# Decayed attention and a gated FFN: one ring of PSUM banks for values and FFN, and RMS weights put into the FFN weights after group 0

## The chip, the cores and the metric

The kernel runs on one core of one Trainium2 chip. The metric is the device time of one execution in microseconds; a kernel is run several times and the median counts.

## The reference

Eight batches of eight heads, 576 tokens, head size 64. Attention adds a decay, the difference of cumulated logs of `f`, to causal scores; its output, put together over the heads, is normalised by its root mean square and goes through a gated FFN.

```python
scores = scale * np.matmul(q, k.transpose(0, 1, 3, 2))
log_f = np.log(np.clip(f, 0.0001, 1.0))
cum = np.cumsum(log_f, axis=-1)
decay = cum[:, :, :, None] - cum[:, :, None, :]
scores = np.where(causal, -1000000000.0, scores + decay)
attn = softmax(scores)                       # over the keys
x = np.matmul(attn, v)                       # -> (8 * 576, 512)
...
rms = np.sqrt(np.mean(x * x, axis=-1, keepdims=True) + 1e-06)
xn = x / rms * rms_g
g = xn @ w_gate                              # 512 -> 1536
silu = g * (1.0 / (1.0 + np.exp(-g)))
out = silu * (xn @ w_val) @ w_out            # 1536 -> 512
```

All inputs and the output are float32; the kernel multiplies in bf16.

## The kernel before, in words

**Tiling.** A batch has four row blocks of 128 tokens and a last one of 64 (`qi` 0 to 4). For each block and each key block up to it, TensorE makes scores of all eight heads into a double PSUM bank (`sc`, 128 x 1024), ScalarE takes the exponent into SBUF (`PT`, or `P` for the last key block), and GpSimd puts zeros over the causal corner (`affine_select`). `values` then multiplies these with `Vs`, the v rows scaled by their decay with the scale itself as a 65th column, into one bank for the even heads and one for the odd heads (`par` 0 and 1). VectorE takes the reciprocal of the 65th column (`rden`) and writes the quotient to `x`. `norm` forms the root mean square on ScalarE and GpSimd and writes `xn` in bf16. The rows are then transposed into `xT`: by TensorE for the first two batches (a PSUM bank and a copy by VectorE per piece), by DMA for the others.

**FFN groups.** A group is 512 rows: the four full blocks of a batch, groups 0 to 7; group 8 collects the eight last blocks (`xTr`). `gate` takes one bank for the product with `wg` and one for that with `wv`, ScalarE makes the tanh (`th`), VectorE makes `ga` from `th` and the first bank, which frees that bank, and then `hT` from `ga` and the second bank, which frees the other. Groups 0 and 1 run piece by piece (one row block, four column chunks in one bank, sixteen 128 x 128 matmuls); the others one column chunk of 128 at a time over 512 rows. `project` adds up twelve matmuls in one bank, ScalarE copies it, SP stores it.

**PSUM.** The eight banks are: four in `sc` (two double banks), one `po` for values, three `ff` for everything else. In batch 0 the odd heads' values use `ff`. When the last score (or the last value) has been taken, the banks of `sc` and `po` are handed to the ring `ff` (`heir`), so the last groups have up to eight.

**RMS weights.** `rms_g` is folded in at two places. Groups 0 and 1 multiply it into their `xT` pieces while copying them from PSUM. After each third of group 1's gates, `weigh` multiplies it into that third of `wg` and `wv` in place (four VectorE multiplies of 128 x 512 for each of the two, called a pack below), for groups 2 to 8. A third of the columns has the index `i`.

**Order.** Nothing is issued in the order of the loops. Every step is a unit with an engine, an assumed duration, a key and dependencies; `Plan.run` plays them through and gives each engine, whenever it is free, the ready unit of the smallest key whose ring slots are free. Keys get a small random offset from a seeded generator. Each engine then runs its units strictly in the planned order. Scores and values are also chained, each to the one before it. `akey` spreads batch b's attention over the FFN of group b - 1, and `qkey` sets the keys of the first two batches by hand. Loads of v, and most of q and k, are issued by GpSimd (POOL), transposes by DMA and stores by SP.

Of the kernel before, what the change touches and what calls it, by code (L numbers as in the profile page):

```python
# [32 lines left out]
class Plan:  # L33

    def __init__(self, rings, fifo, heir):
        self.units, self.fifo, self.heir = [], fifo, heir
        self.free = {name: list(range(n)) for name, n in rings.items()}
        self.left = {name: [] for name in rings}  # L40
# [24 lines left out]
    def end_of(self, u):  # L65
        for h in u.give:
            h.n -= 1
            if h.n == 0:
                if h.ring in self.heir and not self.left[h.ring]:
                    to, slots = self.heir[h.ring]  # L70
                    self.free[to] += slots(h.slot)
                else:
                    self.free[h.ring].append(h.slot)
        for v in u.then:
            v.need -= 1
            if v.need == 0:
                self.ready[v.eng].append(v)

    def run(self):
# [67 lines left out]
def fox_ffn_kernel(ctx, tc, q, k, v, f, moe_w_gate, moe_w_val, moe_w_out, moe_rms_g, out):  # L147
    nc = tc.nc
# [14 lines left out]
    def ring(name, n, shape, dt, pool=sb):  # L163
        return [pool.tile(shape, dt, name=f"{name}{i}") for i in range(n)]

    sizes = dict(qk2=4, qk=12, QT=3, v32=4, Vs=2, PT=8, P4=2, x=6, xn=4, xT=2, xTr=1, hT=2, th=2, ga=2, ores=3,
                 sc=2, po=1, ff=3, hw=8, sw=8)
    T_qk2 = ring("qk2", sizes["qk2"], [128, H, 2, D], BF16)
# [15 lines left out]
    T_sc = ring("sc", sizes["sc"], [128, 2, 512], F32, ps)  # L184
    T_po = ring("po", sizes["po"], [128, 512], F32, ps)
    T_ff = ring("ff", sizes["ff"], [128, GT], F32, ps)
    n_ff, n_sc = sizes["ff"], sizes["sc"]
    T_ff += [t[:, i, :] for t in T_sc for i in range(2)] + T_po

# [15 lines left out]


    P = Plan(sizes, {"v32", "qk", "qk2", "QT", "Vs", "PT", "x", "xn"}, {"sc": ("ff", lambda i: [n_ff + 2 * i, n_ff + 2 * i + 1]),
                     "po": ("ff", lambda i: [n_ff + 2 * n_sc + i])})

# [122 lines left out]
    def load_w(i, key):  # L332
        c0, c1 = i * 512, (i + 1) * 512
        for w, src, nm in ((wg, moe_w_gate, "g"), (wv, moe_w_val, "v")):
            def emit(w=w, src=src):
                nc.gpsimd.dma_start(out=w[:, :, c0:c1], in_=src[:, c0:c1].rearrange("(c p) f -> p c f", p=128))
            Lw[nm, i] = load("POOL", 0.75, (512, 0.0061), key, emit, late=2.6)

    def weigh(i, key, deps):

        c0, c1 = i * 512, (i + 1) * 512
        for w, nm in ((wg, "g"), (wv, "v")):
            def emit(w=w):
                for dc in range(NDC):
                    nc.vector.tensor_scalar_mul(w[:, dc, c0:c1], w[:, dc, c0:c1], rgT[:, dc:dc + 1])  # L345
            Lw[nm, i] = dve(1.14, key, emit, deps)

# [131 lines left out]

    def bank_of(h):  # L480
        return T_ff[h.slot] if h.ring == "ff" else T_po[h.slot]

    hold_x, evac, last_val = {}, {}, [None]

    def values(b, qi, key):
        p0, n = rows(qi)
        hx = hold_x[b, qi] = Hold("x", 1)
        for par in range(2):
            hpo = Hold("ff" if b == 0 and par == 1 and qi < LAST else "po", 1)

# [30 lines left out]
    def norm(b, js, key):  # L521
# [15 lines left out]
        for i, j in enumerate(js):  # L537
# [6 lines left out]
            if g < 2:  # L544
# [9 lines left out]
                def cp(hf=hf, g=g, c=c):  # L554
                    tp = T_ff[hf.slot].bitcast(BF16)[:, 0:512].rearrange("p (c t) -> p c t", t=128)
                    nc.vector.tensor_tensor(T_of[g][hold_xT[g].slot][:, :, c:c + 128], tp, bcast(rgT, 128), ALU.mult)
                pieces[b, j] = dve(0.65, key - 0.02, cp, [t, L_rg], take=[hold_xT[g]], give=[hf])
            else:
# [37 lines left out]
    def gate(g, key, deps, i, pairs):  # L596
# [114 lines left out]
```

## Time and profile before

| | |
|---|---|
| runs | 401.74, 398.55, 401.13 us (median 401.13) |
| profiled execution | 398.83 us, of which the span is 396.7 us |
| TensorE busy | 365.8 us, 92% of the span |
| VectorE, ScalarE, GpSimd busy | 225.0, 237.7, 196.8 us |
| packs of RMS weights (L345) | 12 + 12 multiplies, 10.9 + 6.0 us, from 85.8 to 124.2 us |
| chain that ended last | TensorE 78%, DMA 7%, VectorE 7%, GpSimd 4% |

The profile names engines PE (TensorE), PEld (its weight loads), DVE (VectorE), ACT (ScalarE), POOL (GpSimd) and SP. Times are in microseconds from the start of the span. A busy TensorE is the bound here; idle time of another engine costs something only where TensorE waits for it.

### The profile page before, as it was taken

Reading aid. Unit: us, or ns where it says so; the run is one execution under the profiler, and the core shown is the slowest. Engines: PE = TensorE matmul, PEld = TensorE weight load, DVE = VectorE, ACT = ScalarE, POOL = GpSimd, SP = SyncE. Lnnn points to the kernel's source line nnn. Section 1 sums busy time; section 2 is a strip of 40 time slices with the busy share of each in tenths; the row PEclk is TensorE's granted clock in tenths of the full one; section 3 lists DMA queues with packets and bytes.
Section 4 is the critical chain, followed back from the end, with each engine's and each line's share of the span. In section 5 each row is a group of like instructions: output and inputs, shape, how many; then the busy total and the mean of one; then the engine's idle time right before and its main releaser. Section 6 shows DMA issues by size and latency. Waiting matters only on the chain.

```text
span 396.7 us, 9672 instructions
## 1 busy us (share of the span) xinstructions
PE 365.8 (92%) x3941; PEld 217.4 (55%) x3941; DVE 225.0 (57%) x456; ACT 237.7 (60%) x377; POOL 196.8 (50%) x275
## 2 busy tenths in 40 slices
PE   2668999997699999899999999999999999999995
PEld 1567898785496554554455544554555444444442
DVE  4555787478968555564565555645555554455530
ACT  4655588786647955786677657865885532232212
POOL 8862469997839945695398456841211100000000
PEclk9998999999979999999999999999999999999998
DMA  9999999999829999899799999992120210001004
GB/s 132 189 200 190 199 143 162 176 175 168 141 39 109 187 158 122 103 154 154 78 122 168 161 112 82 190 150 55 32 57 28 55 33 28 26 26 55 26 28 106
DMA packets 133708, 44.83 MB, mean 113 GB/s; under 512 B 122432, under 2 KB 127040, under 8 KB 133664
## 3 DMA queue, kind: packets, MB, share of 16 engines
q0 software_dynamic: 76000, 22.16, 59.2%
q1 hardware_dynamic: 57136, 22.05, 30.7%
q8 instruction: 31, 0.51, 0.6%
q10 hardware_dynamic: 528, 0.00, 0.2%
q14 instruction: 13, 0.11, 0.1%
HBM read 37.90 MB, written 9.44 MB: 119 GB/s over the span
## 4 chain that ended last, share of the span: by engine, by line
PE 78%; DMA 7%; DVE 7%; POOL 4%; issue 2%; ACT 1%; SPq 0%; ACTq 0%; POOLq 0%
PE ff L605 35%; PE ff L630 17%; PE po L498 7%; PE sc L605 6%; PE sc L451 6%; PE sc L630 5%; DMA v<-in_v_dram 4%; DMA xT<-xn 3%; PE po L605 2%; DVE wg L345 1%; DVE wv L345 1%; DVE hT L612 1%; DVE ga L619 1%; POOL qk L303 1%; DVE x L514 1%
## 5 line engine op out<-in xcount | busy, mean ns | idle before, releaser
L469 ACT ACTIVATE PT<-sc 128x1024 bf16<-128x1024 f32 x96 | 95.2, 1018 | 22.6 <-PE sc L451 22.5
L605 PE MATMUL ff<-xT,wg 128*128 128x128 bf16 (+1 forms) x628 | 88.8, 290 | 5.9 <-DVE ga L619 3.2
L605 PE MATMUL ff<-xT,wv 128*128 128x128 bf16 (+1 forms) x636 | 90.7, 288 | 1.0 <-DVE hT L612 0.8
L619 DVE SCALAR_TENSOR_TENSOR ga<-th,ff 128x512 f32<-128x512 f32 x87 | 59.2, 683 | 49.2 <-ACT th L617 48.8
L630 PE MATMUL ff<-wo,hT 128*128 128x512 bf16 x336 | 86.1, 379 | 0.0
L605 PEld LDWEIGHTS <-wg 128*128 128x128 bf16 x720 | 55.9, 102 | 42.4 <-issue 6.3
L617 ACT ACTIVATE th<-ff 128x512 f32<-128x512 f32 x87 | 51.5, 595 | 44.6 <-PE ff L605 32.8
L605 PEld LDWEIGHTS <-wv 128*128 128x128 bf16 x720 | 54.9, 100 | 36.6 <-issue 1.8
L612 DVE SCALAR_TENSOR_TENSOR hT<-ga,ff 128x512 bf16<-128x512 f32 x94 | 63.7, 683 | 18.7 <-PE ff L605 16.7
L630 PEld LDWEIGHTS <-hT 128*128 128x128 bf16 x432 | 40.1, 98 | 45.1 <-issue 1.3
L476 POOL TENSOR_SCALAR_AFFINE_SELECT PT<-PT 128x1024 bf16<-128x1024 bf16 x32 | 35.4, 1106 | 58.0 <-ACT PT L469 57.7
L498 PEld LDWEIGHTS <-PT 128*128 128x128 bf16 x896 | 38.4, 99 | 17.3 <-issue 4.8
L498 PE MATMUL po<-Vs,PT 128*128 128x65 bf16 x856 | 41.1, 196 | 3.2 <-DVE x L514 2.4
L426 POOL TENSOR_TENSOR Vs<-v,decT 128x512 bf16<-128x512 f32 (+1 forms) x30 | 31.7, 1057 | 12.8 <-DMA v<-in_v_dram 12.2
L451 PE MATMUL sc<-QT,KT 64*128 64x128 bf16 (+1 forms) x960 | 34.6, 214 | 3.0 <-ACT PT L469 1.4
L512 DVE RECIPROCAL rden<-po 128x4 f32<-128x4 f32 (+1 forms) x76 | 13.5, 177 | 40.7 <-PE po L498 40.5
L451 PEld LDWEIGHTS <-KT 64*128 64x128 bf16 x960 | 25.0, 97 | 19.4 <-issue 14.9
L530 ACT ACTIVATE junk<-x 128x512 bf16<-128x512 f32 (+1 forms) x40 | 25.1, 627 | 14.7 <-DVE x L514 14.6
L514 DVE TENSOR_TENSOR x<-po,rden 128x256 f32<-128x256 f32 (+1 forms) x76 | 32.1, 423 | 2.6
L326 POOL DMA_DIRECT2D v<-in_v_dram x34 | 30.4, 896 | 0.1
L303 POOL DMA_DIRECT2D qk<-in_q_dram x34 | 30.1, 885 | 0.8 <-POOLq L695 0.8
L542 ACT ACTIVATE xn<-x,rs 128x512 bf16<-128x512 f32 (+1 forms) x40 | 27.2, 714 | 5.4 <-POOL rs L535 5.3
(76 smaller groups left out, 306.1 us busy)
## 6 DMA issues: line engine op xcount, KB each, us to landing
out_dram<-ores SPq DMA_DIRECT2D x32, 256.0 KB, 2.4
v<-in_v_dram POOLq DMA_DIRECT2D x27, 256.0 KB, 5.3
qk<-in_q_dram POOLq DMA_DIRECT2D x26, 128.0 KB, 5.9
qk<-in_k_dram POOLq DMA_DIRECT2D x26, 128.0 KB, 5.7
wg<-in_moe_w_gate_dram POOLq DMA_DIRECT2D x3, 512.0 KB, 15.9
wv<-in_moe_w_val_dram POOLq DMA_DIRECT2D x3, 512.0 KB, 17.4
wo<-in_moe_w_out_dram POOLq DMA_DIRECT2D x2, 768.0 KB, 17.6
v<-in_v_dram SPq DMA_DIRECT2D x5, 256.0 KB, 9.9
```

What stands on the lines that cost most here:

```text
L303: nc.gpsimd.dma_start(out=T_qk[h.slot][0:n, :].rearrange("p (h d) -> p h d", d=D), in_=src[b, :, p0:p0 + n, :].rearrange("h p d -> p h d"))
L426: eng.tensor_tensor(T_Vs[hv.slot][0:n, j, :, 0:D], T_v32[h.slot][0:n, :, :], bcast(dj, D), ALU.mult)
L451: nc.tensor.matmul(t[:, par, c:c + n], lhsT=kt[r, p, kj * 128:(kj + 1) * 128], rhs=qt[r, p, qi * 128:qi * 128 + n], start=True, stop=True)
L469: nc.scalar.activation(T_of_p[hp.slot][:, 0:2 * half].rearrange("p (a c) -> p a c", a=2)[:, :, 0:cols], T_sc[h.slot][:, :, 0:cols], ACT.Ex ...
L476: nc.gpsimd.affine_select(out=d, in_=d, pattern=[[0, 8], [1, n]], compare_op=ALU.is_ge, fill=0.0, base=0, channel_multiplier=-1)
L498: nc.tensor.matmul(po[:, p, :], lhsT=T_of_p[h.slot][:, c:c + 128], rhs=vs[:, kj, 2 * p + par, :], start=(kj == 0), stop=(kj == qi))
L514: nc.vector.tensor_tensor(d, po[:, :, 0:D], bcast(r, D), ALU.mult)
L605: nc.tensor.matmul(T_ff[h.slot][:, c:c + n], lhsT=w[:, dc, fc * 128:(fc + 1) * 128], rhs=xT[:, dc, t0:t0 + n], start=(dc == 0), stop=(dc = ...
L612: nc.vector.scalar_tensor_tensor(hT, in0=three[0], scalar=0.5, in1=three[1], op0=ALU.mult, op1=ALU.mult)
L617: th = act(0.6, key - 0.1, lambda: nc.scalar.activation(T_th[ht.slot], T_ff[hg.slot], ACT.Tanh, scale=0.5), [ug], take=[ht])
L619: a = dve(0.72, key - 0.1, lambda: nc.vector.scalar_tensor_tensor(T_ga[ha.slot], in0=T_th[ht.slot], scalar=1.0, in1=T_ff[hg.slot], op0=ALU ...
L630: nc.tensor.matmul(T_ff[hf.slot], lhsT=T_hT[hold_hT[g].slot][:, fc, j * 128:(j + 1) * 128], rhs=wo[:, fc, :], start=(fc == 0), stop=(fc == ...
```

## The change

Values take their banks from `ff` in all batches, `po` is gone, and `ff` has four banks to the end: nothing is handed over from `sc`. Group 0 alone multiplies `rms_g` into its `xT` pieces; group 1's pieces become plain copies, and the weights are multiplied between groups 0 and 1, each pack as soon as the four gates of group 0 that read it have been issued. The packs' keys move from 1.25, 1.5, 1.75 to 0.75, 1.0, 1.25, their assumed duration from 1.14 to 1.3. The keys of the 64-row blocks of batches 0 and 1 move from -4.8 and -4.2 to 0.3 and 0.9, and the random seed is another one, so that the plan of all engines is drawn anew.

```diff
     def __init__(self, rings, fifo, heir):
...
-                if h.ring in self.heir and not self.left[h.ring]:
-                    to, slots = self.heir[h.ring]
-                    self.free[to] += slots(h.slot)
-                else:
-                    self.free[h.ring].append(h.slot)
+                self.free[h.ring].append(h.slot)
...
-        draw = random.Random(71)
+        draw = random.Random(149)
...
-                 sc=2, po=1, ff=3, hw=8, sw=8)
+                 sc=2, ff=4, hw=8, sw=8)
...
+    PLAIN = 1
...
     def weigh(i, key, deps):
...
-            Lw[nm, i] = dve(1.14, key, emit, deps)
+            Lw[nm, i] = [dve(1.3, key, emit, deps[nm])]
...
     def values(b, qi, key):
...
-            hpo = Hold("ff" if b == 0 and par == 1 and qi < LAST else "po", 1)
+            hpo = Hold("ff", 1)
...
     def norm(b, js, key):
...
-                    nc.vector.tensor_tensor(T_of[g][hold_xT[g].slot][:, :, c:c + 128], tp, bcast(rgT, 128), ALU.mult)
-                pieces[b, j] = dve(0.65, key - 0.02, cp, [t, L_rg], take=[hold_xT[g]], give=[hf])
+                    to = T_of[g][hold_xT[g].slot][:, :, c:c + 128]
+                    if g < PLAIN:
+                        nc.vector.tensor_tensor(to, tp, bcast(rgT, 128), ALU.mult)
+                    else:
+                        nc.vector.tensor_copy(to, tp)
+                pieces[b, j] = dve(0.69 if g < PLAIN else 0.42, key - 0.02, cp, [t, L_rg], take=[hold_xT[g]], give=[hf])
...
     def qkey(b, qi, ahead=0.0):
         if b < 2:
-            return (2 * b - 9 + 0.2 * (START[qi] + ahead)) if qi < LAST else -4.8 + 0.6 * b + 0.04 * ahead
+            return (2 * b - 9 + 0.2 * (START[qi] + ahead)) if qi < LAST else 0.3 + 0.6 * b + 0.04 * ahead
...
-                if g == 1:
-                    weigh(i, 1 + (i * 4 + 4) / 16, [ended[1, i * 4 + j] for j in range(4)])
+                if g == PLAIN - 1:
+                    weigh(i, PLAIN - 1 + (i * 4 + 12) / 16, {"g": [began[g, i * 4 + j] for j in range(4)],
+                                                             "v": [ended[g, i * 4 + j] for j in range(4)]})
```

What this does to the engines' order is shown at three places. The first is VectorE's queue around the middle packs, among group 1's gates. Before (`ff_124` to `ff_126` are the three `ff` banks, `po_123` the values' bank, `hT_113` holds group 1, `x` rows are the values' evacuations):

```order
L512 RECIPROCAL rden_142<-po_123 128x4
L514 TENSOR_TENSOR x_100<-po_123,rden_142 128x4x64
L612 SCALAR_TENSOR_TENSOR hT_113<-ga_117,ff_126 128x4x128
L345 TENSOR_SCALAR wg<-wg,rgT 128x512 x4
L619 SCALAR_TENSOR_TENSOR ga_116<-th_115,ff_124 128x512
L345 TENSOR_SCALAR wv<-wv,rgT 128x512 x4
L612 SCALAR_TENSOR_TENSOR hT_113<-ga_116,ff_125 128x4x128
```

In the changed kernel three of the packs stand at the turn from group 0 to group 1 (`hT_112` holds group 0, the two `COPY` rows are the first plain xT pieces of group 1, `ff_123` is the fourth bank):

```order
L606 SCALAR_TENSOR_TENSOR hT_112<-ga_117,ff_123 128x4x128
L550 COPY xT_110<-ff_125 128x4x128
L550 COPY xT_110<-ff_126 128x4x128
L338 TENSOR_SCALAR wg<-wg,rgT 128x512 x4
L338 TENSOR_SCALAR wv<-wv,rgT 128x512 x4
L613 SCALAR_TENSOR_TENSOR ga_116<-th_114,ff_125 128x512
L338 TENSOR_SCALAR wg<-wg,rgT 128x512 x4
L502 RECIPROCAL rden_141<-ff_124 128x4
L504 TENSOR_TENSOR x_100<-ff_124,rden_141 128x4x64
```

The other three packs stand further ahead, one by one among group 0's gates; behind the last of group 1's gates there is none any more.

The second place is VectorE's queue in the first 40 us, at the scaling of batch 1's fourth v block (`Vs_88<-v_83`), which waits for a load. Before, with the two evacuations of batch 0's fourth block (`x_102`) behind it:

```order
L612 SCALAR_TENSOR_TENSOR hT_112<-ga_117,ff_125 128x4x128
L426 TENSOR_TENSOR Vs_88<-v_83,decT 128x8x64
L427 CAST Vs_88<-decT 128x8
L619 SCALAR_TENSOR_TENSOR ga_116<-th_114,ff_124 128x512
L512 RECIPROCAL rden_141<-po_123 128x4
L514 TENSOR_TENSOR x_102<-po_123,rden_141 128x4x64
```

Now both evacuations stand ahead of it:

```order
L504 TENSOR_TENSOR x_102<-ff_123,rden_141 128x4x64
L606 SCALAR_TENSOR_TENSOR hT_112<-ga_117,ff_126 128x4x128
L502 RECIPROCAL rden_142<-ff_125 128x4
L504 TENSOR_TENSOR x_102<-ff_125,rden_142 128x4x64
L419 TENSOR_TENSOR Vs_88<-v_83,decT 128x8x64
L420 CAST Vs_88<-decT 128x8
L613 SCALAR_TENSOR_TENSOR ga_116<-th_114,ff_124 128x512
```

The third place is the last gates of group 8 on VectorE. Before, the banks come from `ff`, `sc` and `po`:

```order
L619 SCALAR_TENSOR_TENSOR ga_117<-th_114,po_123 128x512
L619 SCALAR_TENSOR_TENSOR ga_116<-th_115,sc_122 128x512
L612 SCALAR_TENSOR_TENSOR hT_112<-ga_117,ff_126 128x512
L612 SCALAR_TENSOR_TENSOR hT_112<-ga_116,ff_124 128x512
```

Now four banks go round:

```order
L613 SCALAR_TENSOR_TENSOR ga_116<-th_114,ff_124 128x512
L613 SCALAR_TENSOR_TENSOR ga_117<-th_115,ff_123 128x512
L606 SCALAR_TENSOR_TENSOR hT_112<-ga_116,ff_125 128x512
L606 SCALAR_TENSOR_TENSOR hT_112<-ga_117,ff_126 128x512
```

More of the change, by code (lines that the diff above doesn't have):

```diff
@@ L33, with __init__ @@
 class Plan:
-    def __init__(self, rings, fifo, heir):
-        self.units, self.fifo, self.heir = [], fifo, heir
+    def __init__(self, rings, fifo):
+        self.units, self.fifo = [], fifo
         self.free = {name: list(range(n)) for name, n in rings.items()}
@@ L184, in fox_ffn_kernel @@
     T_sc = ring("sc", sizes["sc"], [128, 2, 512], F32, ps)
-    T_po = ring("po", sizes["po"], [128, 512], F32, ps)
     T_ff = ring("ff", sizes["ff"], [128, GT], F32, ps)
-    n_ff, n_sc = sizes["ff"], sizes["sc"]
-    T_ff += [t[:, i, :] for t in T_sc for i in range(2)] + T_po
     wg = sb.tile([128, NDC, DF], BF16, name="wg")
@@ L204, in fox_ffn_kernel @@
     rden = [sb.tile([128, 4], F32, name=f"rden{i}") for i in range(2)]
-    P = Plan(sizes, {"v32", "qk", "qk2", "QT", "Vs", "PT", "x", "xn"}, {"sc": ("ff", lambda i: [n_ff + 2 * i, n_ff + 2 * i + 1]),
-                     "po": ("ff", lambda i: [n_ff + 2 * n_sc + i])})
+    P = Plan(sizes, {"v32", "qk", "qk2", "QT", "Vs", "PT", "x", "xn"})
     def pe(dur, key, emit, deps=(), take=(), give=()):
@@ L336, in emit @@
                 nc.gpsimd.dma_start(out=w[:, :, c0:c1], in_=src[:, c0:c1].rearrange("(c p) f -> p c f", p=128))
-            Lw[nm, i] = load("POOL", 0.75, (512, 0.0061), key, emit, late=2.6)
+            Lw[nm, i] = [load("POOL", 0.75, (512, 0.0061), key, emit, late=2.6)]
     def weigh(i, key, deps):
@@ L478, in score_block @@
                 masked[b, qi].append(pool(0.15 + 0.95 * n / 128, key, mk, [e]))
-    def bank_of(h):
-        return T_ff[h.slot] if h.ring == "ff" else T_po[h.slot]
     hold_x, evac, last_val = {}, {}, [None]
@@ L488, in values @@
         for par in range(2):
-            hpo = Hold("ff" if b == 0 and par == 1 and qi < LAST else "po", 1)
+            hpo = Hold("ff", 1)
             def emit(par=par, hpo=hpo):
-                po = bank_of(hpo)[:, 0:4 * 65].rearrange("p (j d) -> p j d", d=65)
+                po = T_ff[hpo.slot][:, 0:4 * 65].rearrange("p (j d) -> p j d", d=65)
                 vs = T_Vs[hold_Vs[b].slot]
@@ L509, in ev @@
             def ev(par=par, hpo=hpo):
-                po = bank_of(hpo)[0:n, 0:4 * 65].rearrange("p (j d) -> p j d", d=65)
+                po = T_ff[hpo.slot][0:n, 0:4 * 65].rearrange("p (j d) -> p j d", d=65)
                 r = rden[par][0:n, :]
@@ L613, in gate @@
         dur = 0.865 if len(pairs) == 1 else 0.9
-        began[g, len([x for x in began if x[0] == g])] = ug = pe(dur, key, lambda: mm(wg, hg), deps + [Lw["g", i]], take=[hg])
-        uv = pe(dur, key + 0.0001, lambda: mm(wv, hv), [ug, Lw["v", i]], take=[hv], give=[hx])
+        began[g, len([x for x in began if x[0] == g])] = ug = pe(dur, key, lambda: mm(wg, hg), deps + Lw["g", i], take=[hg])
+        uv = pe(dur, key + 0.0001, lambda: mm(wv, hv), [ug] + Lw["v", i], take=[hv], give=[hx])
         ended[g, len([x for x in ended if x[0] == g])] = uv
```

## The prediction

> **What bounds the kernel now.** I read the page's first two parts first, then the span in short windows, then the waits and the timeline of the stretch that stands out.
>
> ```profile
> PE 365.8 (92%) x3941; PEld 217.4 (55%) x3941; DVE 225.0 (57%) x456; ACT 237.7 (60%) x377; POOL 196.8 (50%) x275
> ...
> PE   2668999997699999899999999999999999999995
> ```
>
> TensorE is the bound: 396.7 - 365.8 = 30.9 us of the span is all that waits can give back, plus what a lowered clock costs. Two places hold nearly all of it: the first 45 us, and a hole around slices 9 to 12. The windows below cut the hole (stretch, length, busy us of PE, PEld, DVE, ACT, POOL, then the granted clock, DMA share, GB/s).
>
> ```profile
> 84.00:88.00 4.00, 3.74 (x81) 3.45 (x80) 3.81 (x8) 3.35 (x6) 3.82 (x6) 1.00 1.34 177
> 88.00:92.00 4.00, 3.26 (x57) 2.55 (x55) 3.93 (x8) 3.21 (x6) 3.99 (x6) 1.00 1.75 182
> 92.00:96.00 4.00, 2.35 (x18) 1.03 (x16) 3.93 (x8) 1.41 (x2) 3.04 (x5) 1.00 1.46 160
> 96.00:100.00 4.00, 3.96 (x86) 3.77 (x86) 2.29 (x8) 3.77 (x7) 2.29 (x4) 1.00 1.43 141
> 100.00:104.00 4.00, 4.00 (x77) 2.80 (x74) 3.82 (x3) 3.64 (x7) 3.99 (x7) 1.00 1.09 181
> 104.00:108.00 4.00, 1.32 (x20) 0.63 (x17) 4.00 (x5) 1.55 (x3) 3.40 (x6) 0.95 0.47 111
> 108.00:112.00 4.00, 3.19 (x37) 3.02 (x37) 2.80 (x10) 0.60 (x1) 0.00 (x0) 0.50 0.19 57
> 112.00:116.00 4.00, 4.00 (x54) 4.00 (x52) 2.17 (x4) 1.85 (x5) 2.62 (x5) 0.70 0.01 2
> ```
>
> From 84 to 112 TensorE is busy 21.8 of 28 us: 6.2 idle. VectorE is full there. The clock is 0.50 and then 0.70: 3.19 x 0.5 + 4.00 x 0.3 = 2.8 us more. Together **9.0 us**. Who makes it is in the timeline (start, length, engine, line; in brackets the idle before and its releaser).
>
> ```profile
> 100.99 6.84 DVE L345 TENSOR_SCALAR wg<-wg,rgT 128x512 bf16<-128x512 bf16 x4
> 101.39 1.04 POOL L426 TENSOR_TENSOR Vs<-v,decT 128x512 bf16<-128x512 f32 x1
> 107.75 0.67 DVE L619 SCALAR_TENSOR_TENSOR ga<-th,ff 128x512 f32<-128x512 f32 x1
> 108.47 1.86 PE L605 MATMUL ff<-xT,wg 128*128 128x128 bf16 x16 [3.15 <-DVE ga L619]
> ```
>
> A pack of four weight multiplies (L345) holds VectorE for 6.84 us while GpSimd runs its v multiplies; the gate operation (L619) that frees an ff bank is queued behind it, and TensorE waits 3.15 us and restarts at half speed. The other packs:
>
> ```profile
> 85.84 2.54 DVE L345 TENSOR_SCALAR wg<-wg,rgT 128x512 bf16<-128x512 bf16 x4
> 90.59 3.71 DVE L345 TENSOR_SCALAR wv<-wv,rgT 128x512 bf16<-128x512 bf16 x4
> 120.86 1.13 DVE L345 TENSOR_SCALAR wv<-wv,rgT 128x512 bf16<-128x512 bf16 x4
> 120.94 2.40 POOL L303 DMA_DIRECT2D qk<-in_q_dram  x2
> 123.05 1.53 DVE L345 TENSOR_SCALAR wg<-wg,rgT 128x512 bf16<-128x512 bf16 x4
> ...
> L345 DVE TENSOR_SCALAR wg<-wg,rgT x12: 332/375/4528, 85.8 to 124.2; 128x512 bf16<-128x512 bf16 x12
> ...
> PE po L498 <- DVE x L514: 2.4, 3, 1.6
> ```
>
> The same multiply takes 332 or 4528 ns. Four times the short one, overlapped, make a pack of 1.13; what GpSimd does meanwhile sets the rest (beside loads that it issues, 1.13 and 1.53). The single po bank costs 2.4 us in three waits, all of them behind these packs, so they are in the 9.0 already.
>
> The Trainium skill (SBUF — State Buffer, "Who interferes with whom") says that a VectorE instruction in a two-port mode and a GpSimd instruction exclude each other for a whole instruction; the 4528 ns agree with being locked out by several in a row.
>
> **The change, part by part.** (1) The packs leave 84 to 125 us and stand among group 0's gates. Their old hole goes: **-9.0**. They bring back a cost at two new places. For the last three (wg, wv, one gate operation, wg in a row) I take what TensorE has queued after the two xT copies, from these rows (the first two from the chain; a unit's length is the distance to the next start).
>
> ```profile
> 71.19 0.89 PE ff L605 x16
> ...
> 62.46 0.86 PE ff L630 x4
> ...
> 102.08 0.64 PE L451 MATMUL sc<-QT,KT 64*128 64x64 bf16 x32
> 102.65 1.04 PE L630 MATMUL ff<-wo,hT 128*128 128x512 bf16 x4
> 103.52 0.71 PE L498 MATMUL po<-Vs,PT 128*128 128x65 bf16 x16
> 104.07 1.03 PE L630 MATMUL ff<-wo,hT 128*128 128x512 bf16 x4
> ...
> L514 DVE TENSOR_TENSOR x<-po,rden 128x256 f32<-128x256 f32 (+1 forms) x76 | 32.1, 423 | 2.6
> ```
>
> Gate 0.9, scores 0.6, gate 0.9, values 0.55, projection 0.86, and 0.3 of the unit running: 4.1 us until TensorE needs the bank that this gate operation frees; then 1.65 more until it needs the bank behind the third pack. VectorE needs two packs + 0.6 for the first, and a third + 0.6 (the 0.42 above and its reciprocal) for the second. At 1.13 a pack nothing waits; at 3.71 TensorE loses (8.0 - 4.1) + (4.3 - 1.65) = 6.6. The new GpSimd order around there holds mostly q and k loads, two causal masks, and the first v multiply some ten rows later, so I take the mean of 1.13, 1.53 and 3.71, the packs that stood beside loads (the last one beside a mask and one v multiply too): 2.1. Then 4.8 - 4.1 = 0.7 and 2.7 - 1.65 = 1.0: **+1.7**. Bounds 0 and 6.6, or 9.4 with the clock's 2.8.
>
> The first three packs stand one by one among gates, with query copies and gate operations queued behind.
>
> ```profile
> 36.00:66.40 30.40, 27.66 (x533) 24.60 (x531) 23.97 (x47) 21.16 (x32) 19.08 (x25) 1.00 1.44 170
> 60.00:107.40 47.40, 41.73 (x776) 33.08 (x771) 34.98 (x64) 37.07 (x60) 43.55 (x62) 1.00 1.59 164
> 112.00:305.00 193.00, 191.24 (x1950) 102.92 (x1948) 107.86 (x223) 134.06 (x216) 113.53 (x156) 0.99 0.99 116
> 305.00:392.00 87.00, 86.16 (x462) 39.56 (x458) 40.55 (x66) 29.14 (x51) 2.27 (x5) 1.00 0.12 38
> ```
>
> VectorE has 30.4 - 24.0 = 6.4 us free from 36 to 66 and three packs take 3.4 to 6.3: they fit, with hand-overs that get late now and then. **+0.5**, bounds 0 and 3.
>
> (2) VectorE's wait for a v load at 37 us keeps its place in time, but what is queued behind it changes.
>
> ```profile
> 36.50 0.65 PE L498 MATMUL po<-Vs,PT 128*128 128x65 bf16 x16
> 37.23 0.69 DVE L426 TENSOR_TENSOR Vs<-v,decT 128x512 bf16<-128x512 f32 x1 [2.84 <-DMA v<-in_v_dram]
> 38.65 0.65 PE L498 MATMUL ff<-Vs,PT 128*128 128x65 bf16 x16 [1.50 <-DVE ga L619]
> 39.79 1.05 PE L605 MATMUL ff<-xT,wv 128*128 128x128 bf16 x16 [0.49 <-DVE hT L612]
> ```
>
> Now both values banks of that block are emptied ahead of the wait, and TensorE has gates to run until the first gate operation behind it, at about 38.7: half of the 2.0 us goes. **-1.0**, bounds -2.0 and 0.
>
> (3) Group 1's four xT pieces become plain copies; the nearest rows are these.
>
> ```profile
> 20.73 0.69 DVE L556 TENSOR_TENSOR xT<-ff,rgT 128x512 bf16<-128x512 bf16 x1 [0.90 <-PE ff L550]
> 27.79 0.41 DVE L410 COPY QT<-ff 128x512 bf16<-128x512 bf16 x1
> ```
>
> 4 x 0.28 = 1.1 us of VectorE, beside TensorE's work: **0**. Without that cover it is 1.1 at most.
>
> (4) Values no longer wait for the one po bank; FFN gates and values now share four. From 112 to 305 us TensorE is busy 191.2 of 193.0 with three banks for gates, so sharing can win or lose little: 0. After 305 the FFN had up to eight banks and now has four.
>
> ```profile
> L617 ACT ACTIVATE th<-ff 128x512 f32<-128x512 f32 x87 | 51.5, 595 | 44.6 <-PE ff L605 32.8
> L619 DVE SCALAR_TENSOR_TENSOR ga<-th,ff 128x512 f32<-128x512 f32 x87 | 59.2, 683 | 49.2 <-ACT th L617 48.8
> ```
>
> A gate's bank is held 0.86 + 0.60 + 0.68 = 2.1 us plus hand-overs; TensorE comes back to it after four units, 3.4 us. The slack is about 1 us, VectorE is half free (40.6 of 87): **+0.5**, bounds -0.8 (all of today's idle time) and +11.
>
> (5) The last blocks of batches 0 and 1 get a later key, but scores and values run in a fixed chain, so they stay near their place; one key transpose moves behind four others on SP, long before it is needed. New random ties reorder the rest: **0**, bounds -2 and +3. The DMAs are the same in number and size.
>
> (6) Removing a hole presses the other engines together. From 60 to 107.4 us GpSimd is busy 43.6, TensorE 41.7. If TensorE stopped waiting, GpSimd could hold it back by 1.8; today only 0.8 us of TensorE's waits is on it, so half: **+0.9**, bounds 0 and 1.8.
>
> Sum: -9.0 + 1.7 + 0.5 - 1.0 + 0.5 + 0.9 = -6.4. The profiled execution took 398.83, so 392.4. The runs shown lie from 398.55 to 401.74, median 401.13; the four together average 400.1, 1.2 above the profiled one. I add that: **393.6**.
>
> **Rivals.** (A) The packs are starved at their new place too: three packs at the mean of 2.54, 3.71 and 6.84, 4.4 each, make TensorE wait 9.4 - 4.1 = 5.3, then 5.0 - 1.65 = 3.3, and a gap that long halves the clock for 2.8 again. 392.4 - 1.7 + 11.4 = 402, with the offset 403; half of it 398. For it: GpSimd has no free moment there. Against: loads, not v multiplies. By the Trainium skill's section named above, loads issued by GpSimd need the same port for their descriptors, so they would lock VectorE out as well, and the time would be this 403 in place of 393.6; 1.13 and 1.53 beside loads speak against most of it, 3.71 for some.
>
> (B) **Slower**: the four shared banks. If VectorE or ScalarE runs more than the 1 us of slack late, each gate in the tail waits. 23 gates follow the last values; at 0.7 us each that is 16 us, 393.6 + 16 = 410. It decides from 0.33 us a gate, where the 7.5 us to 401.1 are gone. Against it: 191.2 of 193.0 with three.
>
> (C) The hole does not vanish but spreads: VectorE with the new packs (24.0 + 3.4 to 6.3 of 30.4) and GpSimd (43.6 of 47.4) delay gates by their upper bounds, 3 and 1.8 in place of 0.5 and 0.9, and new ties cost 3: 393.6 + 6.4 = 400.
>
> The Trainium skill (TensorE: Matmul & The Clock Gate, "What's actually happening") states an idle window of about 3.4 us before the clock halves; here 3.15 us of idle, with little work around it, was enough, and 1.65 at 93 us was not. A new wait under 2 us would then cost only itself.
>
> **How the numbers follow.** Forecast 0.64 (389 to 397); A 0.13 (398 to 403); C 0.14 (396 to 400); B 0.09 (over 401). Range 388.5 to 401: it leaves out B, a part of A, and a better start. A measurement of this kernel tells about 1% from no change: under 397.1 is faster (the forecast and a part of C: 0.67), 397.1 to 405.1 the same (0.25), above 0.08.
>
> **What would show it.** Right: no TensorE idle over 1 us and no half clock after 60 us; packs from 43 to 75 us of 1.1 to 2.5 each; L345 busy 10 to 13 us against 16.9; TensorE idle about 25 us. Wrong: a pack over 4 us, a wait of TensorE on ga or x over 2 us, idle time over 3 us after the last values, or waits for masks on GpSimd.

## The result and the profile after

The changed kernel takes **387.0 us** (383.7 to 388.5, four runs) against 399.8 us (396.7 to 401.7, four runs) beside it: ratio 0.968, interval 0.958 to 0.977. The forecast was 393.6 us in a range of 388.5 to 401.0: the direction held, but the gain is 3.2% where 1.9% was forecast, and the time lies below the range. The profiled execution took 386.79 us, with a span of 384.8 us (before: 398.83 and 396.7). Medians and ratios below are those of undisturbed runs alone: disturbed were two of four times of e1 (428 and 743 us, its profile among them), two of four of e1b (396 and 539 us), five of ten of e13 (399.5 to 401.1 us) and three of eight of e12 (399.9 to 402.5 us, its profile, 400.3 us, among them).

The page of the changed kernel, busy time of the engines and the rows in 40 slices:

```profile
PE 357.3 (93%) x3896; PEld 212.6 (55%) x3941; DVE 218.3 (57%) x456; ACT 237.1 (62%) x377; POOL 196.9 (51%) x275
...
PE   2679999999999987999999999999999999999994
...
PEclk9999999999999999999999999999999999999998
```

TensorE stays the bound. The dent in slices 10 and 11 (7 and 6 before) is gone and a smaller one stands in 15 and 16 (8 and 7). There are 3896 matmul records for 3941 weight loads: 45 are missing, so the 357.3 is a few us too low. The clock record, which starts at 24.2 us, shows full clock from there to 382.6 us.

The packs in VectorE's timeline of the changed kernel, at their new place:

```profile
43.05 1.33 DVE L338 TENSOR_SCALAR wv<-wv,rgT 128x512 bf16<-128x512 bf16 x4
46.69 1.12 DVE L338 TENSOR_SCALAR wg<-wg,rgT 128x512 bf16<-128x512 bf16 x4
58.31 1.88 DVE L338 TENSOR_SCALAR wv<-wv,rgT 128x512 bf16<-128x512 bf16 x4
62.64 2.45 DVE L338 TENSOR_SCALAR wg<-wg,rgT 128x512 bf16<-128x512 bf16 x4
65.01 1.69 DVE L338 TENSOR_SCALAR wv<-wv,rgT 128x512 bf16<-128x512 bf16 x4
67.22 1.93 DVE L338 TENSOR_SCALAR wg<-wg,rgT 128x512 bf16<-128x512 bf16 x4
```

They take 10.4 us in all, the longest 2.45. These are windows of the kernel before at two places that the prediction did not show in one piece (columns as there):

```profile
28.00:32.00 4.00, 3.32 (x40) 3.03 (x41) 2.82 (x6) 3.34 (x6) 1.59 (x3) 0.63 1.22 197
84.00:112.00 28.00, 21.81 (x361) 17.25 (x360) 24.59 (x44) 17.52 (x28) 20.54 (x30) 0.92 1.10 144
```

The same two windows of the changed kernel, and a third:

```profile
28.00:32.00 4.00, 3.18 (x56) 2.63 (x54) 2.42 (x6) 3.59 (x6) 2.65 (x4) 1.00 1.21 195
84.00:112.00 28.00, 27.39 (x487) 21.41 (x488) 15.02 (x36) 22.67 (x38) 26.07 (x38) 1.00 1.56 163
140.00:152.00 12.00, 7.94 (x68) 3.91 (x67) 4.54 (x8) 5.33 (x8) 8.99 (x12) 1.00 1.26 140
```

From 84 to 112 us TensorE is busy 27.4 us where it was 21.8. At 28 to 32 us the kernel before ran at a mean clock of 0.63, the changed one at 1.00. And there is a new gap at 140 to 152 us, which this timeline of the changed kernel explains:

```profile
140.56 1.04 POOL L419 TENSOR_TENSOR Vs<-v,decT 64x512 bf16<-64x512 f32 x1 [2.83 <-DMA v<-in_v_dram]
...
142.13 0.72 POOL L525 TENSOR_TENSOR rs<-ms,mhalf 128x2 f32<-128x2 f32 x1
...
142.88 0.72 ACT L532 ACTIVATE xn<-x,rs 128x512 bf16<-128x512 f32 x1 [4.27 <-POOL rs L525]
...
144.86 1.02 PE L599 MATMUL ff<-xT,wg 128*128 128x512 bf16 x4 [1.80 <-DVE ga L613]
...
151.08 1.02 PE L599 MATMUL ff<-xT,wg 128*128 128x512 bf16 x3 [2.21 <-DMA xT<-xn]
```

GpSimd waits 2.83 us for a v load (just before, 3.01 us for another). Behind the multiply in its queue stands the reciprocal root (L525), behind that xn on ScalarE, and behind xn both a tanh (so a gate bank comes free late, 1.80 us) and the xT transposes of group 2 (2.21 us).

**The difference by stage.** To compare two orders I cut each trace into stages where TensorE had been given the same amount of work: every weight load counts as long as its matmul (0.056 us for a 128-column gate, 0.215 for 512 columns, 0.030 scores, 0.035 values, 0.06 transposes; 351.7 us in all). Stage A is the first 20 us of work, B goes on to 60, C to 90, D to 140, E to 290, and F is the rest. In the kernel before these end at 44.6, 85.2, 124.8, 176.7, 328.3 and 396.6 us: B holds most of group 0, C the old packs, F the tail. In the changed kernel the cut between C and D falls where TensorE waits (a wait of 0.9 us, with its weight load 1.4); counted from the other end of that wait, C is 29.9 and D 55.8. With the way of cutting, C and D of e11 move by 1.1 us and other lengths by 0.5 or less. Lengths are in us, from one trace each; e12's trace is of an execution of 400.3 us:

| kernel | median | ratio (interval) | A | B | C | D | E | F |
|---|---|---|---|---|---|---|---|---|
| before | 399.8 | | 44.6 | 40.6 | 39.6 | 51.9 | 151.6 | 68.4 |
| changed | 387.0 | 0.968 (0.958-0.977) | 40.3 | 40.8 | 31.4 | 54.4 | 150.5 | 67.3 |
| e2: packs moved, alone | 401.0 | 1.005 (1.001-1.010) | 45.8 | 49.3 | 30.0 | 54.4 | 152.0 | 68.5 |
| e6: rings, alone | 390.5 | 0.977 (0.974-0.980) | 43.1 | 40.5 | 36.7 | 50.4 | 150.5 | 67.4 |
| e13: ties and keys, alone | 397.9 | 0.993 (0.987-0.998) | 44.0 | 43.6 | 36.3 | 52.4 | 151.2 | 69.4 |
| e4: all but the rings | 394.4 | 0.987 (0.981-0.993) | 42.4 | 48.4 | 29.6 | 50.8 | 151.2 | 69.5 |
| e1b: all but the packs | 390.6 | 0.977 (0.972-0.983) | 42.9 | 41.9 | 33.1 | 51.6 | 150.5 | 67.3 |
| e3: all but the ties | 387.2 | 0.969 (0.962-0.975) | 42.7 | 42.6 | 30.1 | 50.8 | 150.5 | 67.3 |
| e5: all but the keys | 385.5 | 0.968 (0.958-0.978) | 41.0 | 41.8 | 31.9 | 50.9 | 150.5 | 67.2 |
| e7: before, packs left out | 388.7 | 0.973 (0.970-0.977) | 45.8 | 40.0 | 29.9 | 51.2 | 151.2 | 68.4 |
| e14: changed, packs left out | 383.8 | 0.962 (0.956-0.967) | 41.2 | 41.1 | 30.3 | 51.0 | 150.5 | 67.3 |
| e8: values one at a time | 388.7 | 0.972 (0.966-0.977) | 41.3 | 42.5 | 33.3 | 51.1 | 150.5 | 67.3 |
| e10: three shared banks | 396.5 | 0.994 (0.992-0.997) | 43.8 | 49.9 | 30.3 | 51.4 | 151.5 | 67.4 |
| e11: packs twice as long | 393.3 | 0.988 (0.982-0.993) | 40.5 | 49.7 | 31.0 | 50.6 | 150.5 | 67.3 |
| e12: v multiplies on VectorE | 396.2 | 0.993 (0.989-0.997) | 45.4 | 41.2 | 40.3 | 51.1 | 152.2 | 68.4 |
| e9: changed, one swap | **383.4** | 0.961 (0.957-0.964) | 41.2 | 40.9 | 30.5 | 50.4 | 150.5 | 67.3 |

### The profile page after: what moved, and what is told of

It is laid out like the page before. It is cut to its first block, busy times and chain, and to the rows that moved or that the text cites. A ratio compares the mean times of both kernels' runs of the same rounds, so it can differ in the third digit from the quotient of the medians.

```text
span 384.8 us, 9635 instructions
## 1 busy us (share of the span) xinstructions
PE 357.3 (93%) x3896; PEld 212.6 (55%) x3941; DVE 218.3 (57%) x456; ACT 237.1 (62%) x377; POOL 196.9 (51%) x275
## 4 chain that ended last, share of the span: by engine, by line
PE 78%; POOL 8%; ACT 4%; DVE 4%; issue 3%; DMA 2%; ACTq 0%; POOLq 0%
PE ff L599 44%; PE ff L624 21%; PE ff L488 7%; PE sc L444 6%; POOL qk L296 2%; DMA xT<-xn 2%; ACT PT L462 2%; POOL Vs L419 1%; POOL v L319 1%; ACT xn L532 1%; DVE wg L338 1%; POOL PT L469 1%; POOL rs L525 1%; DVE wv L338 1%; ACT junk L520 1%
## 5 line engine op out<-in xcount | busy, mean ns | idle before, releaser
L613 DVE SCALAR_TENSOR_TENSOR ga<-th,ff 128x512 f32<-128x512 f32 x108 | 73.8, 685 | 80.5 <-ACT th L611 79.1
L611 ACT ACTIVATE th<-ff 128x512 f32<-128x512 f32 x108 | 64.2, 596 | 75.1 <-PE ff L599 59.9
L624 PE MATMUL ff<-wo,hT 128*128 128x512 bf16 x413 | 105.8, 379 | 0.8
L599 PE MATMUL ff<-xT,wg 128*128 128x128 bf16 (+1 forms) x659 | 96.2, 288 | 6.0 <-DMA xT<-xn 2.2
L606 DVE SCALAR_TENSOR_TENSOR hT<-ga,ff 128x512 bf16<-128x512 f32 x108 | 72.9, 684 | 21.5 <-PE ff L599 18.0
L469 POOL TENSOR_SCALAR_AFFINE_SELECT PT<-PT 128x1024 bf16<-128x1024 bf16 x32 | 35.5, 1110 | 49.7 <-ACT PT L462 49.6
L488 PE MATMUL ff<-Vs,PT 128*128 128x65 bf16 x896 | 42.4, 195 | 2.4 <-POOL PT L469 1.2
L504 DVE TENSOR_TENSOR x<-ff,rden 128x256 f32<-128x256 f32 (+1 forms) x80 | 33.8, 423 | 2.8
L502 DVE RECIPROCAL rden<-ff 128x4 f32<-128x4 f32 (+1 forms) x80 | 14.6, 182 | 36.0 <-PE ff L488 34.7
L629 ACT COPY ores<-ff 128x512 f32<-128x512 f32 x36 | 21.1, 585 | 21.9 <-PE ff L624 20.8
L296 POOL DMA_DIRECT2D qk<-in_k_dram x34 | 29.8, 877 | 3.8 <-DMA wg<-in_moe_w_gate_dram 1.8
```

The costliest lines, as they stand in the source:

```text
L296: nc.gpsimd.dma_start(out=T_qk[h.slot][0:n, :].rearrange("p (h d) -> p h d", d=D), in_=src[b, :, p0:p0 + n, :].rearrange("h p d -> p h d"))
L469: nc.gpsimd.affine_select(out=d, in_=d, pattern=[[0, 8], [1, n]], compare_op=ALU.is_ge, fill=0.0, base=0, channel_multiplier=-1)
L488: nc.tensor.matmul(po[:, p, :], lhsT=T_of_p[h.slot][:, c:c + 128], rhs=vs[:, kj, 2 * p + par, :], start=(kj == 0), stop=(kj == qi))
L599: nc.tensor.matmul(T_ff[h.slot][:, c:c + n], lhsT=w[:, dc, fc * 128:(fc + 1) * 128], rhs=xT[:, dc, t0:t0 + n], start=(dc == 0), stop=(dc = ...
L606: nc.vector.scalar_tensor_tensor(hT, in0=three[0], scalar=0.5, in1=three[1], op0=ALU.mult, op1=ALU.mult)
L611: th = act(0.6, key - 0.1, lambda: nc.scalar.activation(T_th[ht.slot], T_ff[hg.slot], ACT.Tanh, scale=0.5), [ug], take=[ht])
```

## Experiments

**Taking the change apart.** My theory at first (M): moving the packs is the gain. Rivals: the rings (R) or the new ties and keys (T).

e1 and e1b put the packs back and keep the rest (`PLAIN = 2`, and):

```
-                if g == PLAIN - 1:
-                    weigh(i, PLAIN - 1 + (i * 4 + 12) / 16, {"g": [began ...], "v": [ended ...]})
+                if g == 1:
+                    weigh(i, 1 + (i * 4 + 4) / 16, [ended[1, i * 4 + j] for j in range(4)])
```

> The changed kernel with the weight multiplies back between groups 1 and 2 (and group 1's xT pieces scaled again); rings, keys and ties stay changed. Theory M (moving the packs is nearly the whole gain, because it removes the hole at 84 to 112 us; rings and keys give little): the hole of 9 us comes back, 396 us (393 to 399), with packs of 2 us and more near 85 to 125 us and a wait of TensorE on ga of over 2 us there. Theory R (the hole was made by the one po bank as much as by the packs, and four shared banks let TensorE run past slow packs): at most half of it comes back, 389 to 392 us. Theory T (the order of ties and keys made the gain): no change, 385 to 389 us.

385.6 and 389.9 us (ratio 0.970, 0.959 to 0.981); and again, for its profile:

> The changed kernel with the weight multiplies back between groups 1 and 2, once more, for an undisturbed profile: two of its four times were 386 and 390 us, the others disturbed. Theory R (now in front): 386 to 390 us, and the profile shows packs of which some take over 2 us between 80 and 130 us while TensorE has no wait on ga or x over 1 us and no halved clock there. Theory M: a hole of 6 us and more there and 394 to 398 us.

The profiled run took 389.2 us, the other 391.9. M would need 394 and more: it fell. TensorE runs on beside a slow pack, as the timeline of e1b shows:

```profile
96.75 1.95 PE L599 MATMUL ff<-xT,wv 128*128 128x128 bf16 x32
96.79 3.61 DVE L338 TENSOR_SCALAR wg<-wg,rgT 128x512 bf16<-128x512 bf16 x4 [1.09 <-PE ff L599]
...
98.64 0.64 PE L444 MATMUL sc<-QT,KT 64*128 64x64 bf16 x32
...
101.04 0.64 PE L488 MATMUL ff<-Vs,PT 128*128 128x65 bf16 x16 [1.77 <-DVE ga L613]
```

A pack of 3.61 us costs a wait of 1.77. R's sign "no wait over 1 us" was missed; its time (386 to 390) holds the profiled run and just misses the mean of the two, 390.6. Set against the changed kernel, the packs' move is worth 3.6 us on top of the other edits (the two intervals overlap).

e2 moves the packs and nothing else (in the kernel before, `weigh` called in group 0, group 1's pieces copied plainly):

> The kernel before with only the weight multiplies moved between groups 0 and 1 (group 1's xT pieces plain copies); po bank, eight banks in the tail, keys and ties as before. Theory M: 399.8 - 9 = 391 us (389 to 393); what is left to 387 is the start and the tail. Theory R: with the single po bank the packs hurt at their new place as they did at the old one, 395 to 400 us. Theory T: 399 us.

401.0 us: no gain, 1 us above even R's range. Stage C loses its hole (30.0 against 39.6), and B takes it over (49.3 against 40.6). The timeline of e2, packs and TensorE's waits:

```profile
54.99 2.28 DVE L345 TENSOR_SCALAR wv<-wv,rgT 128x512 bf16<-128x512 bf16 x4
...
57.86 0.40 PE L498 MATMUL po<-Vs,PT 128*128 128x65 bf16 x8 [1.13 <-DVE x L514]
...
64.12 1.43 DVE L345 TENSOR_SCALAR wg<-wg,rgT 128x512 bf16<-128x512 bf16 x4
65.94 0.38 PE L550 MATMUL ff<-ident,xn 128*128 128x128 bf16 x4 [1.24 <-DVE xT L560]
66.74 2.34 DVE L345 TENSOR_SCALAR wv<-wv,rgT 128x512 bf16<-128x512 bf16 x4
70.28 0.65 PE L498 MATMUL po<-Vs,PT 128*128 128x65 bf16 x16 [0.41 <-DVE x L514]
```

Packs as short as in the changed kernel (the longest of the six 2.34 us) make TensorE wait, now for po, now for a transpose's bank.

e4 is the changed kernel with the old rings:

```
-                 sc=2, ff=4, hw=8, sw=8)
+                 sc=2, po=1, ff=3, hw=8, sw=8)
...
-            hpo = Hold("ff", 1)
+            hpo = Hold("ff" if b == 0 and par == 1 and qi < LAST else "po", 1)
```

> The changed kernel with the old PSUM rings (po of one bank, three for the FFN, the banks of scores and values handed to the FFN after the last scores); packs, keys and ties stay changed. Theory M: the rings are worth 0 to 3 us, all of it before 50 us and in the tail: 387 to 390 us. Theory R: the single po bank costs most of the gain, 392 to 398 us, seen as waits of TensorE for po on x (L504's line) of over 5 us in sum. The rival that eight banks help the tail: 385 us.

394.4 us: R. B is 48.4, the tail 69.5. R's sign was wrong in part: the waits for po on x are 1.2 us in sum, and the largest wait after the first 6 us, in e4's timeline, is that of a transpose of xn that wants an ff bank, behind a pack:

```profile
63.34 3.65 DVE L345 TENSOR_SCALAR wg<-wg,rgT 128x512 bf16<-128x512 bf16 x4 [0.78 <-PE ff L609]
...
67.37 0.59 PE L550 MATMUL ff<-ident,xn 128*128 128x128 bf16 x4 [3.11 <-DVE xT L560]
```

That pack is longer than any of the changed kernel, so a part of e4's loss in B may be the longer pack's. But e2, whose packs are short, loses as much there.

e6 has the new rings alone:

> The kernel before with only the PSUM rings changed (four banks shared by values and FFN, none handed over in the tail); packs, keys and ties as before. Theory R: nearly the whole gain, 386 to 391 us, no hole at 84 to 112 us, and no halved clock. Theory RT (the rings together with the new keys and ties): half of it, 392 to 396 us. Theory M: 398 to 402 us.

390.5 us, 9.3 less: R's time. But R's sign, no hole, failed: TensorE is busy 24.35 us from 84 to 112, the clock is halved once, and C is 36.7, only 2.9 less than before. The rest of the gain is spread over A (1.5), D (1.5), E (1.1) and F (1.0). The timeline of e6 shows a pack of 4.12 us beside GpSimd's multiplies, and a gate waiting behind it:

```profile
101.67 4.12 DVE L337 TENSOR_SCALAR wv<-wv,rgT 128x512 bf16<-128x512 bf16 x4
...
102.94 1.05 POOL L418 TENSOR_TENSOR Vs<-v,decT 128x512 bf16<-128x512 f32 x1
...
104.08 1.04 POOL L418 TENSOR_TENSOR Vs<-v,decT 128x512 bf16<-128x512 f32 x1
...
105.72 0.68 DVE L608 SCALAR_TENSOR_TENSOR ga<-th,ff 128x512 f32<-128x512 f32 x1
...
106.45 3.03 PE L594 MATMUL ff<-xT,wg 128*128 128x128 bf16 x32 [2.69 <-DVE ga L608]
```

e3 takes the old draw of ties (`random.Random(71)`), e5 the old keys of the last blocks (`-4.8 + ...`), e13 is the kernel before with the new ties and keys:

> The changed kernel with the old draw of ties; nothing else. Theory M: the hole stays away, so no more than 3 us either way, 385 to 390 us; the wait for xT at 145 to 151 us, which costs 3 us in the changed kernel, may go or another may come. Theory T: most of the gain is the draw, 394 to 400 us.

> The changed kernel with the old keys for the last blocks of batches 0 and 1. If the keys do nothing, as the prediction's part (5) has it: 385 to 389 us and a start (work up to the point where TensorE has 20 us of work behind it) of 40 to 43 us. If the keys give the start: a start of 44 us and more and a halved clock near 30 us, 390 us.

> The kernel before with only the new ties and the new keys; rings and packs as before. If the rings give the start: 44 to 46 us there, a halved clock near 30 us, and 398 to 401 us in all. If ties and keys give half of it (the kernel with old rings and all else changed had 42.4 there, the one with the new rings alone 43.1): a start of 42.5 us and 396 to 398 us. The hole between 80 and 115 us stays in both, 8 us and more.

387.2, 385.5 and 397.9 us: alone, ties and keys are worth 1.9 us (by the ratio 0.2 to 1.3%), and under the new rings nothing that shows. T as the reason of the whole gain fell. The start of e13 (44.0, with a halved clock at 32 us) is at the lower end of the first expectation, and its C (36.3) is 6.4 above that of e7 below, not 8. But the edits lean on each other. With the new ties and keys there, the packs' move does bring something under the old rings: e4 against e13 is 3.5 us (the intervals overlap), -6.7 in C and +4.8 in B. The other way round, with the packs moved under the old rings, ties and keys are worth 6.6 us (e2 to e4), in A and D above all. Only the rings are worth much wherever they were tried: 9.3 us alone, 7.3 with ties and keys (e13 to e1b), 7.4 with all else (e4 to the changed kernel).

**Packs left out.** e7 is the kernel before, e14 the changed one, with an empty `emit` in `weigh`, so both leave out the multiply of the weights by `rms_g`; in e14 no other instruction changes its place.

> The kernel before without any multiply of the FFN weights by the RMS weights (this part of the computation is left out); rings, keys and ties as before, and the order of the rest nearly so. If the packs make the hole in the kernel before: 390 to 392 us, no halved clock after 60 us. If the one po bank makes it, whatever VectorE does: 397 to 400 us, with a hole of some us still between 80 and 115 us. Between them (packs and bank together) 393 to 396 us.

> The changed kernel without any multiply of the FFN weights by the RMS weights (this part of the computation is left out); the order of every other instruction is kept. If the packs still cost what the prediction gave them (1.7 + 0.5): 384 to 386 us. If they are free under four shared banks: 386 to 388 us. If they cost 3 us and more: under 384 us.

e7 takes 388.7 us. It gains 11.1 us, 9.7 of it in C, though the one po bank is still there:

```profile
84.00:112.00 28.00, 28.00 (x524) 23.59 (x524) 17.69 (x39) 23.13 (x37) 26.18 (x40) 1.00 1.32 161
```

So the packs make the hole, and the rings set how much of it TensorE feels: of the 9.7 us in C, 6.8 are left with the new rings alone (e6) and 3.2 with the new rings, ties and keys (e1b). e14 takes 383.8 us, 3.3 less than the changed kernel. By its time alone that says that the packs still cost over 3 us; but its trace gains 0.8 us at most in B and C together, less than the 1.4 that the cut leaves open, and the rest is the gap at 140 us, which it lacks.

**What in the rings.** e8 plans each half block's values behind the emptying of the half before (`deps += [last_val[0], last_ev[0]]`); e10 has three shared banks (`ff=3`).

> The changed kernel with one condition more in the planned order: the values of a half block come only after the values half ahead of it has been emptied, in any of the four banks. If the gain of the rings is that two halves run behind each other without waiting for VectorE: 392 to 396 us, as with the old rings. If the gain is that FFN, key and xT transposes get the fourth bank when no values need it: 386 to 389 us.

> The changed kernel with three shared banks in place of four (one bank of PSUM unused). If sharing is what helps (any user takes any free bank): 387 to 391 us. If the fourth bank for FFN and transposes is what helps: back to the old rings with moved packs, 393 to 401 us, with waits of TensorE on ga, hT and x over 5 us in sum from 40 to 75 us.

388.7 and 396.5 us. Two halves back to back are not the point (at most 1.7 us). Three shared banks are no better than one and three: B is 49.9. The waits of e10, TensorE by what it waited for (us in total, times, longest), and from its timeline the longest wait with the pack ahead of it:

```profile
PE ff L488 <- DVE ga L613: 4.7, 4, 2.7
...
PE ff L540 <- DVE ga L613: 1.8, 1, 1.8
...
65.57 3.60 DVE L338 TENSOR_SCALAR wg<-wg,rgT 128x512 bf16<-128x512 bf16 x4 [1.59 <-PE ff L599]
...
69.82 0.95 PE L488 MATMUL ff<-Vs,PT 128*128 128x65 bf16 x16 [2.65 <-DVE ga L613]
```

One of e10's packs takes 3.60 us where the changed kernel's longest takes 2.45, so e10 doesn't separate the missing bank from the longer pack.

e11 does every weight multiply a second time into a spare tile, in the same order:

```
                     nc.vector.tensor_scalar_mul(w[:, dc, c0:c1], w[:, dc, c0:c1], rgT[:, dc:dc + 1])
+                    nc.vector.tensor_scalar_mul(spare, w[:, dc, c0:c1], rgT[:, dc:dc + 1])
```

> The changed kernel with each weight multiply done a second time into a spare tile, right behind the first; the order is the same on every engine. This adds 8 to 12 us of VectorE work to the packs at 43 to 69 us. If four shared banks cover slow packs: under 3 us more, 387 to 390 us. If what counts is that the packs are short at their new place: the added work shows to more than half, 392 to 398 us.

393.3 us, 6.3 more: 8.9 more in B, while D, without the gap at 140 us, has 3.8 less. The packs now take 2.9 to 3.8 us each. Four shared banks bridge the packs of 1.1 to 2.5 us, not these. In e11's windows TensorE is busy 2.04 and 1.30 us of 4, with a halved clock behind each:

```profile
44.00:48.00 4.00, 2.04 (x48) 1.83 (x48) 3.89 (x10) 1.86 (x2) 1.24 (x2) 1.00 1.25 208
48.00:52.00 4.00, 4.00 (x55) 3.76 (x49) 3.86 (x10) 1.94 (x2) 1.81 (x2) 0.57 1.38 212
72.00:76.00 4.00, 1.30 (x14) 0.76 (x13) 3.82 (x12) 0.86 (x1) 0.81 (x1) 0.92 2.32 161
```

**GpSimd's part.** e12 is the kernel before with the v multiplies of batches 2 and 3 on VectorE (`if b < 4` in place of `b < 2`).

> The kernel before with the v multiplies of batches 2 and 3 on VectorE in place of GpSimd. If GpSimd's multiplies are what stretches a pack (one multiply of 4528 ns): all six packs 1.1 to 1.6 us and 393 to 397 us. If VectorE's own load is the trouble: packs as before or the same hole, 399 to 404 us.

Of 24 multiplies the longest is now 1223 ns instead of 4528 (least/median/most ns in e12's groups):

```profile
L345 DVE TENSOR_SCALAR wg<-wg,rgT x12: 336/342/1223, 86.8 to 125.1; 128x512 bf16<-128x512 bf16 x12
L345 DVE TENSOR_SCALAR wv<-wv,rgT x12: 333/344/768, 95.2 to 123.2; 128x512 bf16<-128x512 bf16 x12
```

Three of six packs take 1.13 us, the others 1.9 to 2.3, where 1.1 to 1.6 was expected of all. The time falls by 0.7%, to 396.2 us: that is in the range expected if GpSimd's multiplies stretch the packs (393 to 397), while the packs are not. Where the 0.7% come from isn't shown, since the one trace is of an execution of 400.3 us. There C stays at 40.3: VectorE now waits for the v loads itself, and the one po bank carries that to TensorE:

```profile
104.97 0.69 DVE L426 TENSOR_TENSOR Vs<-v,decT 128x512 bf16<-128x512 f32 x1 [3.09 <-DMA v<-in_v_dram]
...
106.11 1.13 DVE L345 TENSOR_SCALAR wg<-wg,rgT 128x512 bf16<-128x512 bf16 x4
107.16 0.67 DVE L619 SCALAR_TENSOR_TENSOR ga<-th,ff 128x512 f32<-128x512 f32 x1
...
107.96 0.42 DVE L514 TENSOR_TENSOR x<-po,rden 128x256 f32<-128x256 f32 x1
...
108.44 1.04 PE L498 MATMUL po<-Vs,PT 128*128 128x65 bf16 x16 [3.94 <-DVE x L514]
```

**A version without the gap at 140 us.** e9 orders GpSimd's root ahead of the multiply that waits for a load:

```
         r = pool(0.9, key, emit, us + [iden_f])
+        if b >= 2 and js[-1] == 3:
+            r.then.append(scaled[b, LAST])
+            scaled[b, LAST].need += 1
```

> The changed kernel with one swap in GpSimd's order, from batch 2 on: the multiply of a batch's last v block comes after the reciprocal root for blocks 2 and 3. In the changed kernel GpSimd waits 2.83 us for that v load at 140.56 us, the root, xn on ScalarE (4.27 us idle), the xT transposes and group 2's first gates wait behind it, and the stage loses 3.3 us against the others. If that queue is the cause: 383 to 385 us, no wait of TensorE on xT over 1 us at 140 to 152 us. If the loads are late whatever the order: 386 to 388 us, the wait found on another step.

383.4 us (382.6 to 384.6, six runs), the lowest median here. D falls from 54.4 to 50.4, and the list of TensorE's waits has none between 134 and 156 us; GpSimd's timeline in e9:

```profile
138.98 0.71 POOL L525 TENSOR_TENSOR rs<-ms,mhalf 128x2 f32<-128x2 f32 x1
...
140.29 1.04 POOL L419 TENSOR_TENSOR Vs<-v,decT 64x512 bf16<-64x512 f32 x1
```

e5 and e14 still have the multiply ahead of the root and have D of 50.9 and 51.0: their load came in time (in e14 it landed about 6 us after its issue, in the changed kernel 9.6). So the gap does not come in every execution; how often it does was not measured. The interval of e9 overlaps that of the changed kernel, so that the swap makes the kernel faster is not shown.

## Why the prediction was right or wrong

Forecast and measured by stage, on the profiled execution (forecast -6.4, measured -12.0):

| step | forecast | measured |
|---|---|---|
| start: (2) the wait at 37 us | -1.0 | A -4.3 |
| (1) cost at the new place; (6) GpSimd's pace | +2.2; +0.9 | B +0.2 |
| (1) the old hole | -9.0 | C -8.2 |
| not in the sum | 0 | D +2.5 |
| (4) and (5) behind the last pack | 0 | E -1.1 |
| (4) the tail | +0.5 | F -1.1 |

The 5.6 us that were missed are the start (-3.3 against its term), the packs' cost at the new place with GpSimd's pace (-2.9) and E and F (-1.1 and -1.6), less the gap in D (+2.5) and a smaller gain in C (+0.8).

**The old hole (1)** had about the right size: -8.2 here, and packs left out give -9.7 in C. **Its reason was half the truth.** I put the po waits into the packs' 9.0 and gave shared banks nothing, because from 112 to 305 us TensorE was busy 191.2 of 193.0; that stretch holds only two short packs, of 1.13 and 1.53 us. **The step that failed** is this part of (4): the rings alone bring 9.3 us, only 2.9 of them in the hole, and the packs' move alone nothing. That C came out near the forecast is luck in part, as the move needed the other edits for it. The edits do not add up: either shrinks the hole, and under the old rings the move carries most of it to B.

**The cost at the new place** was computed for four shared banks, as it should be: +1.7 and +0.5, measured +0.2 in B, 0.8 at most in B and C by e14. All six packs fell between 1.12 and 2.45 us, inside the 1.1 to 2.5 that were named, with 10.4 us in sum (10 to 13 named). The upper bounds, 6.6 and 9.4, are near what it costs under the old rings: B is 8.4 and 9.3 us longer in e4 and e2 than in e7 (40.0).

**The start (2)** was the largest miss of a size, 3.3 us. I priced the two waits shown from 36 us on and left out the halved clock ahead of them, whose row (0.63 above) was not among mine: 3.41 us at half speed is 1.7 us at most. Rings alone give -1.5 in A, ties and keys alone -0.6, all but the rings -2.2. Kernels with the old rings, ties and keys lie from 44.6 to 45.8, so a split finer than 1 us, and with it the rest of the 3.3, stays open.

**GpSimd's pace (6)** named the right engine at the wrong place: it held TensorE not at 60 to 107 us, but at 140, by late v loads. "No TensorE idle over 1 us" after 60 us was wrong there (1.80 and 2.21). "No half clock" was right.

**The tail**: four banks are not worse than eight; F is 67.2 to 67.4 in every kernel with shared banks, 68.4 to 69.5 without. E shows the same on its longer stretch: 150.5 with four shared banks, 151.2 to 152.2 with the old rings. Rivals A and C, starved packs and a spread hole, did not come at the new place. Rival B, the tail, did not come either; that it would be the risk was argued from 0.7 us a gate that no trace shows.

The 1.2 us that I added for the mean of the runs also went the wrong way: this profiled execution lay 0.2 below its median.

On the clock the forecast leaned on the Trainium skill (TensorE: Matmul & The Clock Gate, "What's actually happening"), which states that the clock halves after an idle window of about 3.4 us, and I concluded that a wait under 2 us costs only itself. The traces differ: the clock record of the kernel before has half speed from 29.06 to 32.48 us, after two waits of TensorE in the 3.41 us ahead:

```profile
27.25 0.38 PE L397 MATMUL ff<-ident,qk 128*128 128x128 bf16 x4 [0.91 <-DVE x L514]
...
28.68 0.40 PE L550 MATMUL ff<-ident,xn 128*128 128x128 bf16 x4 [1.05 <-ACT xn L542]
```

In e11 TensorE was busy 2.04 of the 4 us before the fall at 48 us. Cut on the grid of the clock record, whose changes lie whole multiples of 3.41 us apart, the 15 falls of all traces before the end follow stretches of 3.41 us in which TensorE was busy 0.53 to 1.67 us; none follows one of 1.66 in e13, nor the changed kernel's emptiest, of 1.75, with most of its wait of 2.21 us. The measurement decides: two waits of 1 us close together can cost up to 1.7 us more, and one of 2.2 nothing more; in these traces the busy share of such a stretch decides, with the border near half.

## What to carry to other kernels

A hole behind a slow block on one engine has two causes, the block and the buffers too few to bridge it; price each with the other left as it is and with the other gone, and don't let a stage without the block speak for the buffers. Four PSUM banks that any user may take were worth 7.3 to 9.3 us here against the same number split by user; how long a block they bridge is found by making the block longer, as e11 does. On an engine that works in order, look for what waits for a load ahead of what others wait for.

## What the runs showed of the hardware

The granted clock fell for 3.41 us or 6.83 us at a time in each of the nine traces that have a fall before the end. The same multiply of 128x512 takes 332 to 4528 ns in the kernel before, the long ones beside GpSimd's multiplies; with those of batches 2 and 3 moved away it takes 1223 ns at most (e12). One load of 128 KB landed 6 us after its issue in one run and 9.6 us in another of the same order.
